# Bias and mask of four attention tiles moved to TensorE, with new load order, attention pace and last output block

## Chip, cores and metric

The kernel runs on one core of one Trainium2 chip. The metric is the device time of one execution, in microseconds (us). All runs quoted below are fast (not disturbed). The profile comes from one of these executions. Its span, from the first to the last record, is shorter than the device time that is reported for the same run (354.5 us of 356.26, for instance). Starts of products are read from the traces, where this does not enter.

## The reference

Attention with a sliding window of 128 keys and a linear bias for each head, followed by a gated feed-forward block. The core of it:

```python
rel = pos[:, None] - pos[None, :]                      # 8 batches, 8 heads, 576 positions, 64 per head
slopes = 2.0 ** (-8.0 * (np.arange(H) + 1) / H)
bias = slopes[:, None, None] * (-np.abs(rel))
mask = (rel >= 0) & (rel < 128)
scores = np.where(mask, q @ k.T / sqrt(64) + bias, -1e9)
x = softmax(scores) @ v                                # x: 4608 tokens x 512
g = x @ w_gate                                         # w_gate, w_val: 512 x 1536
out = (g * sigmoid(g) * (x @ w_val)) @ w_out           # w_out: 1536 x 512
```

## The kernel before

The 4608 tokens are nine blocks of 512 for the feed-forward part; the attention makes them in 36 tiles. The first four tiles are computed at once. From there the two parts are interleaved: TensorE's list is 12 pairs of gate and up products for each block (`pg`, `pv`), the output product of the block before (`po`), and between them the attention of the tiles that come next. Three places matter for what follows.

The masks of the attention. A table `m_reg` = exp(-slope x distance), zero outside the window, is made on ScalarE, and VectorE multiplies the exponentials by it:

```python
def first_masks():
    nc.vector.tensor_copy(idf, idm)
    for h in sorted(range(H), key=slot):
        nc.scalar.activation(reg[:, slot(h), :], dist, AF.Exp, scale=-(2.0 ** (-8.0 * (h + 1) / H)))
# ... in scores():
    def act(q4, par):
        o = 4 * q4 + 2 * par
        nc.scalar.activation(e[:, o:o + 2, :], banks[q4][par], AF.Exp, scale=scale)
    def mul(q4):
        o = slice(4 * q4, 4 * q4 + 4)
        nc.vector.tensor_mul(e[:, o, :], e[:, o, :], reg[:, o, :])
```

The pace. After each step of the feed-forward part, as many steps of the attention are emitted as `target` says. One attention step brings its transposes of q and k, its scores, its exponentials, or its product with v into the program. A tile of q or k is loaded some tiles ahead by GpSimd's DMA queue, as its buffer comes free, and then transposed by TensorE through the identity (`pt<-idm,qn`):

```python
while (at := next(steps)) < ALONE:          # ALONE = 8: these feed-forward steps go alone
    ...
for step in steps:
    b1 = 24 + 3 * PRE                       # 24: the first block ends, the second begins
    if step < b1:
        target = base + max(0, step - ALONE) + max(0, step - 16) * (32 - b1 + ALONE) / (b1 - 16)
    elif step < 60:
        target = base + 32 + SECOND * 8 * (step - b1) / (60 - b1)
    ...
    while (n_att < target or done < ready[blk]) and att_step():
        pass
```

The end. Blocks 1 to 7 use Strassen's scheme for their output product, seven products of half size in place of eight; the last block uses the plain form, with a small last store:

```python
for j in range(3):
    for _ in project(NBLK - 1, j, ps_a, "a", 4):
        yield 1.0
yield from last_project(NBLK - 1, 3)        # two halves of 256 columns, stored on two queues
```

The softmax here doesn't subtract the row's maximum and nothing guards it: scores larger than these inputs give would overflow.

## Time and profile before

| | before |
|---|---|
| median of 3 runs | 356.27 us (356.26 to 356.39) |
| span of the profiled run | 354.5 us |
| TensorE busy | 341.5 us, 96% |
| start of the first gate product | 18.38 us |
| start of the fourth gate product (the first with 512 columns) | 26.67 us |
| start of the second block's first gate product | 56.93 us |
| stretches at half clock, from 6.45 us, where the trace's clock record begins, to TensorE's last product | none (clock 1.00) |

The prediction below shows the page and the stretches.

### The profile page before, as it was taken

The page shows a single profiled execution, that of the slowest core. Times are in us where ns is not written, and L with a number is a line of the kernel's source. Part 1 is how long each engine was busy: PE and PEld are TensorE (multiplying, and loading weights), DVE is VectorE, ACT ScalarE, POOL GpSimd, SP SyncE. Part 2 cuts the span into 40 slices and gives each one's busy share as a digit, 9 for nine tenths or more (in the row PEclk, how much of TensorE's full clock was granted, in tenths as well). Part 3 has the DMA queues.
Part 4 walks back from the last instruction along what each step waited for, and adds up shares of the span by engine and source line. Part 5 has one row for each costly group of instructions (what it writes and reads, how often), then busy time and mean ns, then how long its engine had stood idle before and what let it go on. Part 6 is the DMA issues. An engine that isn't in the chain of part 4 may idle for free.

```text
span 354.5 us, 7261 instructions
## 1 busy us (share of the span) xinstructions
PE 341.5 (96%) x2765; PEld 197.5 (56%) x2765; DVE 273.4 (77%) x599; ACT 178.9 (50%) x355; POOL 106.9 (30%) x132
## 2 busy tenths in 40 slices
PE   7889999999999999999999999999999999999995
PEld 4684555444456655565456555664665566556643
DVE  4867976997987799678986998799878965975540
ACT  6845584555555455665556455455444323332321
POOL 8966655544848445544300100000000000000000
PEclk9999999999999999999999999999999999999999
DMA  9999999999999999999995513311022101101114
GB/s 152 170 186 187 141 176 155 99 147 137 157 142 196 146 158 163 157 167 153 165 62 105 83 39 32 88 33 58 17 75 61 44 2 59 62 0 62 41 42 96
DMA packets 157763, 37.34 MB, mean 105 GB/s; under 512 B 147232, under 2 KB 153248, under 8 KB 157728
## 3 DMA queue, kind: packets, MB, share of 16 engines
q0 software_dynamic: 116224, 18.62, 79.8%
q1 hardware_dynamic: 41056, 17.97, 27.6%
q8 instruction: 21, 0.34, 0.4%
q10 hardware_dynamic: 448, 0.30, 0.3%
q14 instruction: 14, 0.11, 0.1%
HBM read 37.91 MB, written 9.44 MB: 134 GB/s over the span
## 4 chain that ended last, share of the span: by engine, by line
PE 73%; DVE 16%; ACT 7%; issue 3%; DVEq 0%; ACTq 0%
PE pv L369 20%; PE pg L369 20%; PE po L489 14%; PE av L320 4%; DVE uu L384 4%; DVE hT L391 3%; PE ps L255 3%; PE po L410 3%; DVE ex L264 3%; PE p L489 2%; ACT ex L260 2%; PE px L346 2%; ACT tt L383 2%; ACT exc L287 2%; DVE x L323 1%
## 5 line engine op out<-in xcount | busy, mean ns | idle before, releaser
L369 PE MATMUL pg<-xT,wg_sb 128*128 128x512 f16 (+2 forms) x464 | 116.0, 365 | 0.6 <-DVE uu L384 0.3
L369 PE MATMUL pv<-xT,wv_sb 128*128 128x512 f16 (+2 forms) x464 | 114.5, 364 | 0.8 <-DVE uu L384 0.4
L383 ACT ACTIVATE tt<-pg 128x512 f16<-128x512 f32 (+2 forms) x110 | 65.5, 596 | 85.2 <-PE pg L369 81.8
L384 DVE SCALAR_TENSOR_TENSOR uu<-tt,pg 128x512 f16<-128x512 f16 (+2 forms) x109 | 73.4, 674 | 34.6 <-ACT tt L383 33.9
L391 DVE TENSOR_TENSOR hT<-uu,pv 128x512 f16<-128x512 f16 (+2 forms) x110 | 74.0, 673 | 7.1 <-PE pv L369 2.2
L369 PEld LDWEIGHTS <-wv_sb 128*128 128x128 f16 x464 | 42.8, 98 | 37.4 <-issue 3.3
L369 PEld LDWEIGHTS <-wg_sb 128*128 128x128 f16 x464 | 42.5, 98 | 36.1 <-issue 3.5
L260 ACT ACTIVATE ex<-ps 128x512 f16<-128x512 f32 x96 | 50.2, 605 | 10.1 <-PE ps L255 10.1
L169 POOL DMA_DIRECT2D va<-in_v_dram x40 | 34.1, 856 | 53.0 <-PE av L320 36.9
L175 POOL DMA_DIRECT2D qn<-in_q_dram x39 | 33.6, 864 | 24.4 <-DMA qT<-qn 14.8
L175 POOL DMA_DIRECT2D kn<-in_k_dram x39 | 33.2, 859 | 25.7 <-DMA kT<-kn 18.4
L264 DVE TENSOR_TENSOR ex<-ex,m_reg 128x1024 f16<-128x1024 f16 x48 | 32.6, 687 | 10.3 <-ACT ex L260 10.3
L489 PEld LDWEIGHTS <-hT 128*128 128x128 f16 x336 | 31.8, 98 | 15.5 <-issue 3.6
L489 PEld LDWEIGHTS <-S 128*128 128x128 f16 x252 | 23.9, 98 | 11.8 <-issue 2.9
L323 DVE TENSOR_TENSOR x<-av,rec 128x256 f16<-128x256 f32 x72 | 29.0, 420 | 0.6
L489 PE MATMUL po<-T,hT 128*128 128x256 f16 x168 | 23.1, 272 | 0.5
L489 PE MATMUL po<-T,S 128*128 128x256 f16 x168 | 23.0, 273 | 0.6 <-ACT p5s L507 0.6
L287 ACT ACTIVATE exc<-psc 128x512 f16<-128x512 f32 x40 | 21.4, 608 | 3.4 <-PE psc L283 3.4
L347 ACT COPY xT<-px 128x512 f16<-128x512 f16 x24 | 14.1, 586 | 14.9 <-PE px L346 14.8
L320 PEld LDWEIGHTS <-ex 128*128 128x128 f16 x384 | 18.4, 97 | 4.9 <-issue 0.7
L320 PE MATMUL av<-va,ex 128*128 128x65 f16 x384 | 20.4, 193 | 0.5
L410 PE MATMUL po<-wo_sb,hT 128*128 128x512 f16 x84 | 19.7, 379 | 0.0
(74 smaller groups left out, 291.0 us busy)
## 6 DMA issues: line engine op xcount, KB each, us to landing
out_dram<-osb SPq DMA_DIRECT2D x32, 256.0 KB, 2.8
va<-in_v_dram POOLq DMA_DIRECT2D x32, 128.0 KB, 7.5
qn<-in_q_dram POOLq DMA_DIRECT2D x31, 128.0 KB, 8.2
kn<-in_k_dram POOLq DMA_DIRECT2D x31, 128.0 KB, 8.1
wo_sb<-in_moe_w_out_dram POOLq DMA_DIRECT2D x2, 768.0 KB, 9.3
wg_sb<-in_moe_w_gate_dram POOLq DMA_DIRECT2D x2, 512.0 KB, 10.5
wv_sb<-in_moe_w_val_dram POOLq DMA_DIRECT2D x2, 512.0 KB, 11.8
out_dram<-osb SPq DMA_DIRECT2D x6, 128.0 KB, 2.4
```

Source lines behind the costliest of these rows:

```text
L169: nc.gpsimd.dma_start(va[rank][p0:p1, :, 0:D], src)
L175: nc.gpsimd.dma_start(t_[p0:p1], src)
L260: nc.scalar.activation(e[:, o:o + 2, :], banks[q4][par], AF.Exp, scale=scale)
L264: nc.vector.tensor_mul(e[:, o, :], e[:, o, :], reg[:, o, :])
L320: nc.tensor.matmul(av[:, j, :], w, val, start=(n == 0), stop=(n == len(todo) - 1))
L323: nc.vector.tensor_mul(x[:, 4 * half:4 * half + 4, :], av[:, :, 0:D], rec.broadcast_to([P, 4, D]))
L369: nc.tensor.matmul(ps[:, c0:c1], w[:, kb, ms], xT[n][:, kb, c0:c1], start=(kb == 0 and c0 == 0), stop=(kb == NKB - 1 and c1 == 512), skip_ ...
L383: nc.scalar.activation(tt, pg[:, c0:c1], AF.Tanh, scale=0.5)
L384: nc.vector.scalar_tensor_tensor(out=uu, in0=tt, scalar=one if (n, m) == PIN else 1.0, in1=pg[:, c0:c1], op0=ALU.add, op1=ALU.mult)
L391: nc.vector.tensor_mul(hT[n][:, m, c0:c1], acted[(n, m)][1][:, c0:c1], pv[:, c0:c1])
L410: nc.tensor.matmul(po, hT[n][:, m, j * P:(j + 1) * P], wo_sb[:, m, :], start=(i == 0), stop=(i == NMB - 1))
L489: nc.tensor.matmul(dst, a[:, m, cols], b[:, m, :], start=(start and m == 0), stop=(m == HM - 1), skip_group_check=True)
```

## The change

The intent is to take the mask products off VectorE between 11 and 19 us. For the first four tiles the bias (with the window mask as a very large distance) is added to the scores in PSUM by a product of the identity with a bias table. With that come further edits: the copies of `xT` of these tiles go from ScalarE to VectorE, dummy products and repeated transposes go, the tables `m_reg` are made later, loads are put in a new order, the attention's pace between the first and the second block is made smoother, and the last block gets the seven products too.

```diff
+    bias = hpool.tile([P, H, 256], FP16, name="bias", tag="hT")
     def first_masks():
+        for n, h in enumerate(by_slot):
+            to, by = bias[:, slot(h), :], -(2.0 ** (-8.0 * (h + 1) / H)) / scale
+            if n % 2:
+                nc.vector.tensor_scalar_mul(to, dist, by)
+            else:
+                nc.scalar.mul(to, dist, by)
+    def later_masks(n, many):                              # the m_reg tables, two by two, later
 ...
+                for par in range(2 if early_tile else 0):
+                    o = 4 * q4 + 2 * par
+                    nc.tensor.matmul(two[par], idm, bias[:, o:o + 2, :], start=True, stop=False)
 ...
-    loaded = 9
-    for a0 in (0, 6):
-        nc.gpsimd.dma_start(wo_sb[:, a0:a0 + 6, :], wo2[:, a0:a0 + 6, :])
+    nc.gpsimd.dma_start(wo_sb[:, 6:12, :], wo2[:, 6:12, :])
+    load_qk(9)
+    nc.gpsimd.dma_start(wo_sb[:, 0:6, :], wo2[:, 0:6, :])
+    load_v(9)
+    loaded = 10
 ...
-                target = base + max(0, step - ALONE) + max(0, step - 16) * (32 - b1 + ALONE) / (b1 - 16)
+                target = base + 1.5 * max(0, step - ALONE) + max(0, step - 16)
 ...
-        for j in range(3):
-            for _ in project(NBLK - 1, j, ps_a, "a", 4):
-                yield 1.0
-        yield from last_project(NBLK - 1, 3)
+        ends = [strassen(NBLK - 1, t) for t in range(2)]
+        for t in 7 * (0, 1):
+            next(ends[t])
+            yield 0.75
```

The pace line: between steps 8 and 24 both forms emit 32 attention steps. The old one has emitted 8 of them by step 16 and 24 in the last 8 steps; the new one 12 by step 16 and 20 after it.

More of the change, by code (lines that the diff above doesn't have):

```diff
@@ L27 @@
 IDLE = {("k", 0): 0, ("q", 0): 2}
-REPEAT = {("q", 1): 4, ("k", 1): 2, ("q", 2): 4}
+REPEAT = {("q", 1): 4, ("k", 1): 2}
 FIRST = 4
@@ L43, in make_distance @@
     u = np.arange(2 * P)[None, :] - np.arange(P)[:, None]
-    return np.where((u >= 0) & (u < WIN), u, 30000).astype(np.float32)
+    return np.where((u >= 0) & (u < WIN), u, 16000).astype(np.float32)
 @with_exitstack
@@ L88 @@
     reg = consts.tile([P, H, 256], FP16, name="m_reg")
+    bias = hpool.tile([P, H, 256], FP16, name="bias", tag="hT")
+    by_slot = sorted(range(H), key=slot)
     def first_masks():
         nc.vector.tensor_copy(idf, idm)
-        for h in sorted(range(H), key=slot):
+        for n, h in enumerate(by_slot):
[5 more added lines that the diff above has]
+    def later_masks(n, many):
+        for h in by_slot[n:n + many]:
             nc.scalar.activation(reg[:, slot(h), :], dist, AF.Exp, scale=-(2.0 ** (-8.0 * (h + 1) / H)))
@@ L198, in transposed @@
         t_ = (natk if name == "k" else natq).pop(rank)
-        for _ in range(REPEAT.get((name, rank), 2) if rank < FIRST else 1):
+        for _ in range(REPEAT.get((name, rank), 1)):
             for j in range(4):
@@ L240, in scores @@
         if p == 3:
-            return scores_128(s, p, p, (s, p), reg[:, :, 0:P])
+            return scores_128(s, p, p, (s, p), reg[:, :, 0:P], i < FIRST)
         ks = (9 * s + p) % NK
         banks = []
+        early_tile = i < FIRST
         e = epool.tile([P, H, 256], FP16, name="ex", tag="ex", bufs=4)
@@ L255, in products @@
                         nc.tensor.matmul(two[par][:, j, :], kT[rows, ks, pair, :],
-                                         qT[rows, p:p + 2, pair, :], start=(j == 0), stop=(j == 1))
+                                         qT[rows, p:p + 2, pair, :], start=(j == 0 and not early_tile),
+                                         stop=(j == 1))
         def act(q4, par):
@@ L262, in mul @@
         def mul(q4):
+            if early_tile:
+                return
             o = slice(4 * q4, 4 * q4 + 4)
@@ L267, in scores, with scores_128 @@
                 [lambda: act(1, 0)], [lambda: act(1, 1), lambda: mul(1)]]
-    def scores_128(s, kt, qt, key, m):
+    def scores_128(s, kt, qt, key, m, early_tile=False):
         ks = (9 * s + kt) % NK
@@ L279, in products @@
             banks.extend(ps_a.tile([P, 4, P], FP32, name="psc", tag="a") for _ in range(2))
+            for par in range(2 if early_tile else 0):
+                nc.tensor.matmul(banks[par].rearrange("k (a b) q -> k a b q", a=2), idm,
+                                 bias.rearrange("k (a par b) q -> k a par b q", a=2, par=2)
+                                 [:, :, par, :, 0:P], start=True, stop=False)
             for j in range(4):
@@ L283, in products @@
                     nc.tensor.matmul(banks[par][:, j, :], kT[rows, ks, j, :], qT[rows, qt, j, :],
-                                     start=(j == 0), stop=(j == 3))
+                                     start=(j == 0 and not early_tile), stop=(j == 3))
         def act(par):
@@ L290, in scores_128 @@
         return [[products], [lambda: act(0)],
-                [lambda: act(1), lambda: nc.vector.tensor_mul(e, e, m)]]
+                [lambda: act(1), lambda: early_tile or nc.vector.tensor_mul(e, e, m)]]
     xs = {}
@@ L302, in weighted @@
             av = pool.tile([P, 4, D + 1], FP32, name="av", tag=tag)
-            if 0 < i < FIRST:
-                for _ in range(2):
-                    nc.tensor.matmul(av.rearrange("p j d -> p (j d)")[:, 0:256], idle[:, 0:P],
-                                     idle[:, 0:256], start=True, stop=True)
             todo = []
@@ L346, in x_transposed @@
             nc.tensor.transpose(pt[:, kb, :], x[:, kb * P:(kb + 1) * P], idm if i < FIRST else idm2)
-        nc.scalar.copy(dst, pt)
+        if i < FIRST:
+            nc.vector.tensor_copy(dst, pt)
+        else:
+            nc.scalar.copy(dst, pt)
     PIN = (1, 0)
@@ L403, in rows_of, with store @@
         return [(0, 128, n * S + j * P)]
+    def store(n, j, osb, c0=0, c1=512, two=False):
+        for i, (p0, p1, r0) in enumerate(rows_of(n, j)):
+            (nc.scalar if two and i else nc.sync).dma_start(out[r0:r0 + p1 - p0, c0:c1],
+                                                            osb[p0:p1, c0:c1])
     def project(n, j, pool, tag, bufs):
@@ L414, in project @@
                 nc.scalar.mul(osb, po, 0.5)
-                for p0, p1, r0 in rows_of(n, j):
-                    nc.sync.dma_start(out[r0:r0 + p1 - p0, :], osb[p0:p1, :])
+                store(n, j, osb)
             yield
-    def last_project(n, j):
-        osb = opool.tile([P, DM], FP32, name="osb", tag="osb")
-        for half in range(2):
-            c = slice(half * DM // 2, (half + 1) * DM // 2)
-            po = ps_a.tile([P, DM // 2], FP32, name="po", tag="a", bufs=4)
-            for m in range(NMB):
-                nc.tensor.matmul(po, hT[n][:, m, j * P:(j + 1) * P], wo_sb[:, m, c],
-                                 start=(m == 0), stop=(m == NMB - 1))
-            if half == 0:
-                nc.scalar.mul(osb[:, c], po, 0.5)
-            else:
-                nc.vector.tensor_scalar_mul(osb[:, c], po, 0.5)
-            for i, (p0, p1, r0) in enumerate(rows_of(n, j)):
-                (nc.sync if i == 0 else nc.scalar).dma_start(out[r0:r0 + p1 - p0, c], osb[p0:p1, c])
-            yield 1.5
     HM = NMB // 2
@@ L479, in strassen @@
         cols = slice(t * P, (t + 1) * P)
-        po = ps_f.tile([P, 2, HC], FP32, name="po", tag="po", bufs=1)
+        end = n == NBLK - 1
+        pool, tag, bufs = (ps_a, "a", 4) if end and t else (ps_f, "po", 1)
+        po = pool.tile([P, 2, HC], FP32, name="po", tag=tag, bufs=bufs)
         p2 = ps_a.tile([P, HC], FP32, name="p2", tag="a")
         top, low = (opool.tile([P, DM], FP32, name="osb", tag="osb") for _ in range(2))
-        p1s = supool.tile([P, HC], FP32, name="p1s", tag="p1s", bufs=1)
-        p5s = supool.tile([P, HC], FP32, name="p5s", tag="p5s", bufs=1)
-        u2s = supool.tile([P, HC], FP32, name="u2s", tag="u2s", bufs=1)
+        if end and t:
+            spare = [opool.tile([P, DM], FP32, name="osb", tag="osb") for _ in range(2)]
+            p1s, p5s, u2s = spare[0][:, 0:HC], spare[0][:, HC:DM], spare[1][:, 0:HC]
+        else:
+            p1s, p5s, u2s = (supool.tile([P, HC], FP32, name=i, tag=i, bufs=1)
+                             for i in ("p1s", "p5s", "u2s"))
         def product(dst, a, b, start=False):
@@ L510, in strassen @@
         half_plus(low[:, HC:DM], X, p5s)
+        if end and t:
+            store(n, t + 2, low, HC, DM, True)
         yield
@@ L513, in strassen @@
         half_plus(top[:, HC:DM], Y, u2s)
+        store(n, t, top, 0, DM, end)
         yield
         product(X, A22, T4)
-        nc.scalar.mul(low[:, 0:HC], X, 0.5)
-        for j, osb in ((t, top), (t + 2, low)):
-            for p0, p1, r0 in rows_of(n, j):
-                nc.sync.dma_start(out[r0:r0 + p1 - p0, :], osb[p0:p1, :])
+        if end:
+            nc.vector.tensor_scalar_mul(low[:, 0:HC], X, 0.5)
+        else:
+            nc.scalar.mul(low[:, 0:HC], X, 0.5)
+        store(n, t + 2, low, 0, HC if end and t else DM, end)
         yield
@@ L546, in ffn @@
                         weight_sums(m // 2 - 1)
-                if 0 < n < NBLK - 1 and m >= 9:
+                if n > 0 and m >= 9:
                     sums(n, m - 9)
@@ L611, in first_tiles @@
         val(0, 0, early[(0, 0, "v")][0], 0, 384)
+        later_masks(0, 2)
         gate(0, 1, early[(0, 1, "g")][0], 0, 384)
@@ L650 @@
     load_w(256, 512)
+    load_w(512, 768)
     load(4)
     load_qk(5, "q")
-    load_w(512, 1024)
+    load_w(768, 1024)
     load_qk(5, "k")
@@ L694, in everything @@
                     nc.scalar.copy(idm2, idm)
+                if at in (1.0, 3.0, 4.0):
+                    later_masks(2 * (1, 3, 4).index(at) + 2, 2)
         for step in steps:
```

## The prediction

> **What bounds the kernel now.** I first read the page's list of engines and its slices, then the stretches of the span, then the chain of waits at the start and at the end. The page:
>
> ```profile
> PE 341.5 (96%) x2765; PEld 197.5 (56%) x2765; DVE 273.4 (77%) x599; ACT 178.9 (50%) x355; POOL 106.9 (30%) x132
> ...
> PE   7889999999999999999999999999999999999995
> ...
> DVE  4867976997987799678986998799878965975540
> ```
>
> TensorE is busy almost everywhere; only its first three slices (some 9 us each) and the last are not full. So a change pays by what it takes off TensorE's list of work, by ending TensorE's waits in the first 60 us, or by shortening the tail. The table of stretches (columns: length, then busy time and count of each engine, clock, DMA) says where the waits are:
>
> ```profile
> 10.00:20.00 10.00, 8.32 (x144) 6.72 (x142) 8.80 (x23) 7.59 (x16) 9.02 (x12) 1.00 2.06 172
> 20.00:30.00 10.00, 9.12 (x117) 7.14 (x113) 6.53 (x17) 4.92 (x12) 5.80 (x8) 1.00 1.82 181
> ...
> 50.00:60.00 10.00, 9.26 (x80) 4.68 (x79) 6.87 (x16) 6.08 (x12) 5.25 (x6) 1.00 2.21 160
> 60.00:80.00 20.00, 19.73 (x151) 9.64 (x150) 19.42 (x43) 11.56 (x23) 9.23 (x11) 1.00 1.80 127
> ```
>
> From 10 to 20 us VectorE is busier (8.80) than TensorE, whose 8.32 includes dummy products. I also added up, from the start of each product to the start of the next, what exceeds the usual distance for its size: about 4 us in 0 to 20 us[...], 1.6 in 20 to 30, 0.3 in 30 to 40, 1.1 in 40 to 50, 1.6 in 50 to 60, and only some 7 us in the other 290 us. The chain of waits, start, length, work:
>
> ```profile
> 13.04 0.42 DVE qT L207
> 13.47 1.20 DVE ex L264 x2
> 14.67 0.10 DVE rec L322
> 14.77 0.02 issue
> 14.80 0.42 DVE x L323
> ...
> 16.10 1.20 DVE ex L264 x2
> 17.30 0.11 DVE rec L322
> 17.41 0.02 issue
> 17.43 0.44 DVE x L323
> 17.86 0.05 issue
> 17.91 0.39 PE av L306 x2
> ```
>
> Here VectorE does the mask products (ex, 1.20 us a tile) between the copies and the normalisation, and TensorE waits. That is what the change aims at. At the end the chain is TensorE alone:
>
> ```profile
> 340.15 7.77 PE po L410 x36
> 347.92 2.63 PE po L426 x24
> ```
>
> so the last block's output product is 7.77 + 2.63 = 10.40 us of exposed TensorE time, and the span ends 3.9 us after it (a VectorE copy, a store, the closing).
>
> [...]216 ns from start to start at 512 columns, 109 at 256, 56 at 128. [...]two 512-column products at 5.2 us took 0.85 us together, 427 ns each. [...]the page shows 605 for ex, and 0.52 us from start to start. [...]
>
> **The change part by part.**
> (1) Masks. Away from VectorE: three tiles at 1.20 us and one at 0.6, 4.2 us, all between 11 and 19 us. To VectorE come four bias products[...] and four xT copies of 0.42 us (1.7 us), taken from ScalarE. On TensorE 14 products of 512 columns come, 14 x 0.216 = 3.0 us; away go 12 dummies x 0.109 = 1.3 us and, since the q/k transposes are repeated less, 24 x 0.056 = 1.3 us. Net +0.4 us in a stretch with idle time.
> With these rows I walked the order of the changed kernel forward. q1 is transposed at 7.5 us as before; the first ex starts at 9.7 (9.52 before), because two bias products stand before it. Then ScalarE is the bound: 12 ex x 0.52 us, to 16.0, and the last exc at 17.3 (18.3 before). The third tile's x is ready at about 18.3, the fourth's at 20.3.
> (2) The weights. TensorE reaches the first gate product at 16.7, but the up-projection weights were issued at 10.80 and took 7.0 us to land: 17.8 us. The loads ahead of them are unchanged, so TensorE waits about 0.9 us there. From 17.8 its own work runs on (first three gate/up pairs, the fourth tile): I get the start of the fourth gate product (first of 512 columns) at about 24.2 us; before it was 26.67. Gain at this point 2.4 us.
> (3) The mask tables move. Eight exps (2.56 us in all) and four copies (about 0.55 each) stood between 4.4 and 9.3 us on ScalarE, under the loads. They now stand among the tanh of the first pairs, at 22 to 30 us. My walk has the third pair's tanh at 26.0 to 26.5 and its VectorE product done at 27.2; the fourth up product needs that PSUM buffer and was at 28.02 before. So only about 1.3 of the 2.4 us survive here. At 32 to 37 us ScalarE has caught up, and I get 1.8 us.
> (4) Loads. The total ahead of the tile loads at 29 to 40 us is the same, only reordered (a quarter of the weights goes ahead of the fifth tile). The q tile that is transposed at 42.4 us landed at 40.1 (issued 30.08, 10.0 us under way). The new order wants it at about 38.5. TensorE then waits some 1 us, unless the load comes sooner. Gain after this: 1.0 us.
> (5) Smoother attention from 40 to 60 us. Before, the attention steps were pressed together there; waits for x and PSUM cost 2.7 us. Now more of them come early, and the first output product comes after two gate pairs. I give this 0.9 us of the 2.7.
> (6) Last block with seven products. 14 x 6 = 84 products of 256 columns at 0.109 us, 9.16 us, for 10.40: 1.24 us less, all exposed. VectorE gets 12 sums of 0.34 us in the last three pairs; the S2 sum should be ready at 342.2 in old times against 342.8 for its use. I take 0.2 us off for a delayed buffer. The store at the end is as small as before (two pieces of 64x256 on two queues), so the tail stays at 3.9 us.
> Sum: 1.0 + 0.9 + 1.0 = 2.9 us at the low reading of (4); if the load does not hold it, 1.8 + 0.9 + 1.0 = 3.7. Between them, weighted toward the upper because VectorE's work falls too: 3.4 us, so 356.3 - 3.4 = **352.9 us**.
>
> **The rivals.**
> A. The early gain is eaten entirely: landings set the pace to 40 us, and the mask tables hold tanh. For it: the DMA slices are full to 190 us, and the landings in (2) and (4) are within 1 to 2 us of their use. Against: the weights for the ninth pair (37.1) still come before I need them (37.8). Then only (6) stays: 355.1 us.
> B. TensorE falls back to half clock, since the dummies are gone. [...]Against: bias products fill the same gaps, and no gap in my walk is over 1 us. It would make 354.5 to 357.
> C. The stalls of 40 to 60 us vanish and the early 2.4 us survive in full: 2.4 + 2.5 + 1.2 = 6.1, 350.2 us. For it: this was presumably tuned; from 20 to 60 us VectorE and ScalarE are below 90% busy.
> D. VectorE becomes the bound from 60 to 80 us, where it has 19.42 of 20 us. If blocks arrive earlier there but VectorE's own work is the same, part of the gain is handed back. [...]353.5 us.
>
> **Range and chances.** A and B bound it above, C below; I keep a bit inside A and C: 350.6 to 355.1 us. Faster by over 2% means under 349.1, more than even C gives: 6%. Slower by over 2% means over 363.4: nothing but a stalled load chain does it, 1%.
>
> **What will show it.** (1) right: no ex product on VectorE before 25 us, and ScalarE's twelve ex nearly without gaps from 9.7 to 16. (2) right: TensorE idle before the first up product until about 17.8. (3) right: the chain between 22 and 30 us goes through ScalarE's tanh behind m_reg. (4) right: a wait of TensorE before the q transposes at about 38 us. (5): excess in 40 to 60 us under 2 us. (6): the last 84 products take 9.2 us, the tail 3.9. The prediction is wrong if products of 512 columns at 10 to 24 us take 427 ns (B), if the fourth gate product starts at 26 us or later (A), or if the 60 to 340 us stretch, 280 us before, itself changes by more than 1 us, which nothing in my sum provides for.

The sum: it came to 1.0 + 0.9 + 1.0 = 2.9 us, or 1.8 + 0.9 + 1.0 = 3.7 with the other reading of (4), was set at 3.4 between them by the author's estimate, and gave 356.3 - 3.4 = 352.9 us. Rival B's 354.5 to 357 us rested on a price for a stretch at half clock. The 216, 109, 56 and 427 ns of TensorE's products and the 605 ns of `ex` are from the trace of the kernel before.

## More of the kernel before

One more view is needed later: TensorE's instructions in order of time where the second block begins. The columns are start, length, engine, line, operation, what is written from what, and how many were merged; a bracket would say how long the engine had been idle before and on what.

```profile
53.82 1.89 PE L410 MATMUL po<-wo_sb,hT 128*128 128x512 f16 x8
...
56.93 1.02 PE L369 MATMUL pg<-xT,wg_sb 128*128 128x512 f16 x4
...
60.38 1.03 PE L369 MATMUL pg<-xT,wg_sb 128*128 128x512 f16 x4
...
61.41 0.61 PE L202 MATMUL pt<-idm,qn 128*128 128x128 f16 x8
```

Read it as an order: output products of the first block, then five groups of gate and up products of the second, and only then, at 61.41 us, the transposes of the q tiles 9 and 10. The load of tile 10 landed at 57.46 us, nearly 4 us earlier. Nothing waits there, but only because of where the scheduler put these transposes.

## The result, and the profile after

| | before | after |
|---|---|---|
| median | 356.3 us (356.26 to 356.39, 4 runs) | 362.44 us (360.52 to 362.84, 4 runs) |
| ratio to before | 1 | 1.0161, 95% interval 1.0124 to 1.0198 |
| span of the profiled run | 354.5 us | 361.0 us |
| mean granted clock of the profiled run | 1.00 | 0.991 |

A ratio is the mean time of one kernel's fast runs over that of the other's fast runs in the same rounds, so it is not quite the ratio of the medians quoted. The change costs 1.6%: within the class "same" of 2%, but on the wrong side, and outside the predicted range of 350.6 to 355.1 us.

First the page of after, list of engines and slices:

```profile
PE 344.2 (95%) x2767; PEld 198.5 (55%) x2767; DVE 279.5 (77%) x619; ACT 177.2 (49%) x357; POOL 108.3 (30%) x134
...
PE   7999995999999999999999999999999999999994
...
PEclk9999996999999999999999999999999999999999
```

TensorE's early slices are fuller than before: the aim was met. But the seventh slice (54 to 63 us) has a 5, and the row of the granted clock has a 6 in the same place, where before it was full.

To see where the time came from, I compared the start of the same gate or up product, counted from the first, in both traces (after minus before):

| product | before | after | difference |
|---|---|---|---|
| first of block 0 | 18.38 | 17.53 | -0.85 |
| fourth gate | 26.67 | 25.41 | -1.26 |
| three quarters of block 0 | 40.48 | 41.15 | +0.67 |
| first of block 1 | 56.93 | 59.43 | +2.50 |
| a quarter of block 1 | 62.87 | 70.06 | +7.19 |
| start of block 2 | | | +6.65 |
| last | 339.77 | 346.27 | +6.50 |

(Between such points other work may have moved to the other side of the product, so only from block 2 on, where both orders have done the same, is a difference all time.) From block 2 to the last product nothing changes. Everything happens before 70 us. TensorE in order of time in after:

```profile
54.49 0.28 PE L364 MATMUL px<-idm,x 128*128 128x128 f16 x2 [0.34 <-DVE x L341]
58.60 0.61 PE L214 MATMUL pt<-idm,qn 128*128 128x128 f16 x4 [3.83 <-DMA qn<-in_q_dram]
59.01 0.63 PE L436 MATMUL po<-wo_sb,hT 128*128 128x512 f16 x1
59.43 1.91 PE L390 MATMUL pg<-xT,wg_sb 128*128 128x512 f16 x4
61.14 1.91 PE L390 MATMUL pv<-xT,wv_sb 128*128 128x512 f16 x4
62.84 1.76 PE L390 MATMUL pg<-xT,wg_sb 128*128 128x512 f16 x4
64.44 1.03 PE L390 MATMUL pv<-xT,wv_sb 128*128 128x512 f16 x4
```

The transposes of q tile 10 now stand ahead of the second block's first gate product. Before, they came after its fifth group. The tile landed at 58.56 us, about as late as before (57.46), and TensorE waited 3.83 us for it. The gate products of 59.43 did not pass the transposes in this trace, though ScalarE's last copy of `xT` before them had ended at 55.40 us. Then a second loss follows: four products of 512 columns take 1.71 us from start to start (59.43 to 61.14) in place of 0.86. That is the half clock: the granted clock is 0.50 there. In stretches of 3.41 us, a length that comes back in the traces below (columns: length; busy time and count of TensorE, its weight loads, VectorE, ScalarE, GpSimd; granted clock; share of the DMA engines and GB/s):

```profile
54.10:57.51 3.41, 0.34 (x4) 0.11 (x2) 1.26 (x4) 1.04 (x2) 1.13 (x2) 1.00 2.42 154
57.51:60.92 3.41, 2.32 (x9) 1.14 (x10) 0.42 (x1) 0.00 (x0) 2.85 (x4) 0.50 2.48 154
60.92:64.33 3.41, 3.41 (x9) 1.18 (x8) 1.94 (x4) 0.60 (x1) 1.26 (x2) 0.50 3.18 153
```

The stretch with 0.34 us of work was followed by two at clock 0.50. TensorE worked in them from 58.60 to 64.33, 5.73 us, of which half, 2.87 us, is loss. With the wait that makes 3.83 + 2.87 = 6.70 us, near the 6.65 at block 2 (the early gain and other small waits are in that number too; a cleaner comparison follows with q10_first). The runs of after seem to differ by the same thing. Only that of 362.78 us was profiled, with two such stretches and a mean clock of 0.991. The mean clocks of the others (0.995 for the run of 360.52 us, 0.991 for 362.10, 0.986 for 362.84) would fit one, two and three; but a mean can also hold half clock from after TensorE's last product (best6's trace has 1.00 from 337 to 348 us, but 0.98 from 330 to 353.6, and its products end at 349.4), so this is not shown.

The chain of waits (start, length, what) shows the smaller points of the prediction as well:

```profile
24.90 1.22 ACT m_reg L105 x4
26.12 0.49 ACT tt L404
26.62 0.02 issue
26.64 0.70 DVE uu L405
...
27.38 1.04 PE pv L390 x4
...
30.45 10.20 DMA qn<-in_q_dram
...
40.70 0.40 PE pt L214 x4
...
46.98 11.58 DMA qn<-in_q_dram
```

Four mask tables hold back the third pair's tanh, and the fourth up product, which needs its PSUM buffer, starts at 27.38 us. Then the chain goes through two loads of q: the one that lands at 40.65 costs TensorE only 0.31 us, the one that lands at 58.56 costs 3.83.

At the end the chain is TensorE again, and shorter than the 7.77 + 2.63 us of before:

```profile
346.65 1.31 PE po L502 x12
347.96 1.31 PE p L502 x12
349.27 6.70 PE po L502 x60
...
355.99 0.42 DVE osb L533
```

That is 1.31 + 1.31 + 6.70 = 9.32 us for 84 products. But the last store landed 3.36 us after this last copy (356.41 to 359.77), where before it took 2.22 (351.01 to 353.23). Ten stores with the 1 MB of the whole block are issued between 353.78 and 356.67 us. So the tail after TensorE grew from 3.9 to 5.05 us and took the gain back.

### The profile page after: what moved, and what is told of

The parts are those of the page before. It is cut to its first block, busy times and chain, and to the rows that moved or that the text cites. A ratio compares the mean times of both kernels' runs of the same rounds, so it can differ in the third digit from the quotient of the medians.

```text
span 361.0 us, 7293 instructions
## 1 busy us (share of the span) xinstructions
PE 344.2 (95%) x2767; PEld 198.5 (55%) x2767; DVE 279.5 (77%) x619; ACT 177.2 (49%) x357; POOL 108.3 (30%) x134
## 4 chain that ended last, share of the span: by engine, by line
PE 76%; DVE 8%; DMA 6%; ACT 5%; issue 2%; POOL 0%; DVEq 0%; ACTq 0%
PE pg L390 22%; PE pv L390 21%; PE po L502 16%; DMA qn<-in_q_dram 6%; PE av L338 4%; PE ps L271 3%; PE p L502 3%; DVE hT L412 2%; DVE uu L405 2%; ACT ex L277 2%; PE px L364 2%; ACT tt L404 2%; PE po L436 1%; PE pt L214 1%; DVE ex L283 1%
## 5 line engine op out<-in xcount | busy, mean ns | idle before, releaser
L390 PE MATMUL pg<-xT,wg_sb 128*128 128x512 f16 (+2 forms) x464 | 117.5, 369 | 0.3 <-DVE xT L366 0.2
L390 PE MATMUL pv<-xT,wv_sb 128*128 128x512 f16 (+2 forms) x464 | 116.2, 367 | 0.9 <-DVE uu L405 0.5
L502 PEld LDWEIGHTS <-hT 128*128 128x128 f16 x384 | 36.4, 98 | 16.2 <-issue 3.4
L283 DVE TENSOR_TENSOR ex<-ex,m_reg 128x1024 f16<-128x1024 f16 x42 | 28.8, 687 | 9.6 <-ACT ex L277 9.6
L502 PEld LDWEIGHTS <-S 128*128 128x128 f16 x288 | 27.4, 98 | 12.3 <-issue 2.9
L502 PE MATMUL po<-T,S 128*128 128x256 f16 x192 | 26.0, 273 | 0.6 <-ACT p5s L520 0.6
L502 PE MATMUL po<-T,hT 128*128 128x256 f16 x192 | 26.1, 272 | 0.4
L271 PE MATMUL ps<-qT,kT 64*128 64x256 f16 x192 | 17.5, 272 | 0.6 <-DVE qT L219 0.5
L368 ACT COPY xT<-px 128x512 f16<-128x512 f16 x20 | 11.7, 586 | 10.0 <-PE px L364 9.9
```

Of the source, the lines that this page charges most:

```text
L271: nc.tensor.matmul(two[par][:, j, :], kT[rows, ks, pair, :], qT[rows, p:p + 2, pair, :], start=(j == 0 and not early_tile), stop=(j == 1))
L390: nc.tensor.matmul(ps[:, c0:c1], w[:, kb, ms], xT[n][:, kb, c0:c1], start=(kb == 0 and c0 == 0), stop=(kb == NKB - 1 and c1 == 512), skip_ ...
L502: nc.tensor.matmul(dst, a[:, m, cols], b[:, m, :], start=(start and m == 0), stop=(m == HM - 1), skip_group_check=True)
```

## The experiments

**Theory P (pace).** The new pace line alone puts q tile 10's transposes ahead of the second block. The wait and the half clock after it are all of the loss. **Rival L (loads).** The new load order makes tile 10 late. **Rival E (early part).** The bias products, or dummies that are gone, changed something that costs time later. **For the end:** the seven products gain on TensorE what the crowd of stores loses. Each edit below is against the changed kernel unless it says otherwise; all results were correct.

### pace_old: the old pace line in the changed kernel

```diff
-                target = base + 1.5 * max(0, step - ALONE) + max(0, step - 16)
+                target = base + max(0, step - ALONE) + max(0, step - 16) * (32 - b1 + ALONE) / (b1 - 16)
```

> The changed kernel with one line undone: the pace at which attention steps are handed out in the first block is the old one. In this build the transposes of q tile 10 stand on TensorE after the first gate and up products of the second block again, as in the kernel before. Theory (q10's place in TensorE's order is the cause: 4.0 us of waiting for its load, then about 2.7 us lost to the half clock): no wait over 1 us between 50 and 60 us, 512-column products never slower than 216 ns after 10 us, time 355.2 +- 0.8 us. Rival (the moved mask tables or the load order are the cause): 361 us or more.

Measured: 358.5 us (356.73 to 359.15), ratio 1.0057 (1.003 to 1.0085). The wait for tile 10 is gone, but the time isn't back. TensorE in order of time:

```profile
55.45 0.59 PE L436 MATMUL po<-wo_sb,hT 128*128 128x512 f16 x2 [2.02 <-DMA wo_sb<-in_moe_w_out_dram]
```

With the old pace the output products of the first block come here, and they need `wo_sb`, whose first half (`0:6`) the new load order had put behind the q and k of tile 9. So a second wait, of 2.02 us, came into place, and in the profiled run a stretch of half clock (56.17 to 59.58). The run of 356.73 us, with a mean clock of 0.999, had none of that length. The old pace with the new load order gives a wait too, only for another load. The size that I expected was missed because I had looked at q tile 10 alone.

### both_old: old pace and old end of the load list

```diff
+    loaded = 9
+    for a0 in (0, 6):
+        nc.gpsimd.dma_start(wo_sb[:, a0:a0 + 6, :], wo2[:, a0:a0 + 6, :])   # in place of the five new lines
-                target = base + 1.5 * max(0, step - ALONE) + max(0, step - 16)
+                target = base + max(0, step - ALONE) + max(0, step - 16) * (32 - b1 + ALONE) / (b1 - 16)
```

> The changed kernel with both the old pace of the attention steps and the old end of the load list; what stays is the bias through the identity, the moved mask tables, the earlier weight quarter and the seven products at the end. Theory (the pace line puts q tile 10 too early, the load order pushes the output weights back; nothing else costs): no wait over 1 us from 45 to 65 us, no half clock, third block 1 to 1.5 us earlier than before, end product 1.1 us shorter but the stores after it 1.1 us longer, time 355.0 +- 0.6 us. Rival (the mask part costs too): 357 us or more.

Measured: 355.75 us (355.3 to 356.22), ratio 0.9982 (0.9967 to 0.9996), just above what was expected (354.4 to 355.6). There is a wait of 0.69 us for `wo_sb`, and no half clock. The product-by-product difference to before is -1.14 us at the fourth gate product and -0.70 from block 1 on, where 1 to 1.5 us had been expected. So the early part of the change, bias on TensorE included, is worth a little; rival E falls.

### loads_late_old: only the old end of the load list, new pace kept

The edit is the first half of the one above.

> The changed kernel with the end of the load list put back (both halves of the output weights, then tile 9 as a whole and tile 10). TensorE's order around 54 us is the same as in the changed kernel in this build. Theory (the order on TensorE decides, the loads only say how long the wait is): q tile 10 still lands at 57.5 to 58.6 us, time 361 to 362.8 us. Rival (the reordered loads are the cause): 356 us or less.

Measured: 362.75 us (362.06 to 363.75), ratio 1.0187 (1.0168 to 1.0205). The waits for tile 10 (3.67 us) and the half clock (58.14 to 64.97) are there, with smaller waits for the k and q tiles 9 (0.33 and 0.64 us). With the old loads tile 10 landed at 59.18 us, later than in after (58.56) and than I expected, so the new load order did not make it late. Rival L falls.

### before_pace: the kernel before with the new pace line alone

```diff
 (against the kernel before)
-                target = base + max(0, step - ALONE) + max(0, step - 16) * (32 - b1 + ALONE) / (b1 - 16)
+                target = base + 1.5 * max(0, step - ALONE) + max(0, step - 16)
```

> The kernel before with the pace line alone changed. In this build q tile 10 is transposed ahead of the second block's first gate product. Theory (the pace line by itself brings the wait): TensorE waits 2 to 4 us for that tile at 54 to 58 us, half clock for one or two windows after it, time 360 +- 1.5 us. Rival (the pace line does harm only after the faster start): 356.2 +- 0.6 us.

Measured: 361.7 us (361.67 to 361.98), ratio 1.015 (1.0135 to 1.0165): one line brings nearly the whole loss, a little more than the expected 358.5 to 361.5 us. TensorE in order of time:

```profile
58.35 0.61 PE L202 MATMUL pt<-idm,qn 128*128 128x128 f16 x4 [1.90 <-DMA qn<-in_q_dram]
58.75 1.91 PE L369 MATMUL pg<-xT,wg_sb 128*128 128x512 f16 x4
```

The same transposes ahead of the same gate products, a wait for the same tile, and products at half clock (55.62 to 62.45, 6.83 us). The loss is put together differently, though: the wait for tile 10 is shorter, and three waits stand before it, of 0.79 us for VectorE's `x` and of 0.85 and 0.44 us for the k and q tiles 9. The transposes of tile 9 begin here at 54.79 us, in before at 56.74. The 3.41 us in which these three waits lie (52.21 to 55.62, 39% busy) were the last at full clock. From block 2 on every product is 5.4 us late. Theory P holds in both directions: put into the good kernel the line gives the loss, taken out together with its load order it removes it.

### q10_first: new pace kept, tile 10 of q loaded earlier

The edit leaves TensorE's order as it is, and only lets the load start sooner. It tells whether the order by itself costs, or the order together with a late load.

```diff
     def load(rank):
-        load_qk(rank)
+        load_qk(rank, "k" if rank == 10 else "kq")
 ...
     load_qk(9)
+    load_qk(10, "q")
```

> The changed kernel with TensorE's order kept word for word, but q tile 10 is loaded right after tile 9, ahead of the second half of the output weights, so that it should land near 52 us instead of 58.56. Theory (that one landing is what TensorE waits for): the wait at 54.6 us goes, clock stays full, time 355.7 +- 0.8 us. Rival (the place in the order disturbs by itself, PSUM or the copies behind it): 360 us or more.

Measured: 356.54 us (356.12 to 356.92), ratio 1.001 (0.9995 to 1.0025). TensorE in order of time, at the place of the 3.83 us:

```profile
54.42 0.39 PE L214 MATMUL pt<-idm,qn 128*128 128x128 f16 x4
54.89 0.39 PE L436 MATMUL po<-wo_sb,hT 128*128 128x512 f16 x1
55.26 1.02 PE L390 MATMUL pg<-xT,wg_sb 128*128 128x512 f16 x4
```

No wait, no half clock. The load landed at 50.80 us, and the time is at the upper edge of what was expected. One load issued earlier gives back 5.9 us of median, and 6.65 - 0.28 = 6.37 us at block 2, against the 6.70 of the account above (0.26 of the 6.37 were there at the first gate product already, 17.27 against 17.53 us). What is left is that this kernel is 0.28 us behind before at block 2, while both_old is 0.70 ahead. Between 30 and 50 us q10_first has three single waits that both_old does not have: 0.48 us (for a copy of `qT`, at 33.98), 0.38 (for the q tile that lands at 40.5) and 0.31 (for an exponential, at 43.16). So the smoother pace has a second, smaller cost: it asks for things a little before they are ready. I did not test this one by itself.

### dum5: dummy transposes in front of the wait

Twenty dummy transposes ahead of the wait were to keep the clock up without touching the wait.

```diff
+        if i == 7:
+            for _ in range(5):
+                for kb in range(NKB):
+                    nc.tensor.transpose(pt[:, kb, :], idle[:, kb * P:(kb + 1) * P], idm2)
```

> The changed kernel with 20 dummy transposes (1.1 us) into the same PSUM tile shortly before the wait, so that the wait for q tile 10 remains[...]. Theory (the loss is 4.0 us of waiting and 2.7 us of half clock after it): the wait stays to about 58.5 us, products after it take 216 ns, time 359.7 +- 0.6 us. Rival (the half clock is only a shadow of the wait and costs little): 362 us.

Measured: 361.47 us (361.18 to 361.74), ratio 1.0146. A miss, nearer to the rival's 362 us. The dummies were done before the wait began, which stayed at 3.73 us, and one stretch of 3.41 us, cut as below, had no work of TensorE at all:

```profile
55.20:58.61 3.41, 0.00 (x0) 0.00 (x0) 0.42 (x1) 0.63 (x2) 1.88 (x3) 1.00 2.43 154
```

The clock was 0.50 all the same, but for 3.41 us (58.61 to 62.03, 92% busy) in place of 6.83. The time is 1.0 us below that of after. But how these stretches lie to the wait differs from run to run (the last at full clock begins at 54.10 us in after, with 0.34 us of work, and at 55.20 here, with none), so it is not shown that the dummies spared the second one. What the run does show is that work ahead of this wait of 3.73 us did not keep the clock up; work inside the wait was not tried.

### seven_only: the kernel before with the seven products of the last block

The edit is the last-block part of the diff above, with its buffers and stores.

> The kernel before with the last block's seven products and their stores alone. Theory (TensorE's gain at the end is given back by stores that all fall into the last 3.4 us): the products take 1.1 us less, the last store lands 1.1 us later after them, time 356.2 +- 0.4 us. Rival (the prediction: the tail stays): 355.1 us.

Measured: 356.08 us (355.98 to 356.14), ratio 0.9991 (0.9976 to 1.0005), as expected. From the start of the last up product to TensorE's end it takes 9.69 us, in place of 10.77, and the last store lands 3.40 us after the last copy in place of 2.22. The gain of 1.1 us and the loss of 1.2 cancel. So the crowd at the end is of this part's making, and has nothing to do with the rest of the change.

### best3: a first try at a better version

Old pace, `wo_sb` in the order of its use, all eight mask tables right after the fourth tile, and the two chains of the end no longer mixed.

```diff
+            if i == FIRST - 1:
+                later_masks(0, 8)            # in place of the calls among the first tanh
-        for t in 7 * (0, 1):
+        for t in (0, 1, 0, 1) + 5 * (0,) + 5 * (1,):
+    for a0 in (6, 0):                        # and the old pace line
```

> The changed kernel with the old pace, the output weights' second half first and both ahead of tile 9, the mask tables made in ScalarE's idle time from 18 us on, and the first two of seven products interleaved but then one pair of row tiles finished ahead of the other, so that its stores leave 3 us earlier. Theory: no wait over 1 us, full clock, fourth up product 0.8 us earlier than in the changed kernel, tail 4.2 us instead of 5.0, time 353.6 +- 0.8 us. Rival (the tail is not set by the crowd of stores): tail 5 us, 354.5 us or more.

Measured: 358.5 us (357.96 to 359.11), ratio 1.0054: a miss. With all eight tables there, the scheduler moved the four copies that follow them ahead of the first tanh too. ScalarE was late for the first pair (its first tanh began at 22.67 us), and this stretch went by:

```profile
22.52:25.93 3.41, 1.69 (x23) 1.21 (x21) 2.59 (x7) 1.85 (x6) 2.69 (x4) 1.00 2.12 169
```

TensorE was busy for half of it, without any long gap (the longest 1.35 us), and the clock was 0.50 in the next 3.41 us (25.93 to 29.34). The unmixed end took 12.2 us on TensorE (341.04 to 353.21) for 9.2 us of work: its products wait for the copies of those before (0.31 us for `p5s`, 0.35, 0.57 and 0.52 for `osb`). The tail after TensorE was 4.13 us, as expected (4.2): with stores that leave earlier it is shorter than the 5.05 us of after, so the crowd of stores set it there.

### seven_early: stores of the end issued as soon as each quarter is done

Against the kernel before, with the seven products:

```diff
         half_plus(top[:, 0:HC], p2, p1s)
+        if end:
+            store(n, t, top, 0, HC, True)
 ...
-        store(n, t + 2, low, 0, HC if end and t else DM, end)
+        store(n, t + 2, low, 0, HC if end else DM, end)
```

> The kernel before with the seven products in the last block, and with finished quarters stored as soon as they are ready: the left half of the top tiles after the second product, the right half of the low ones after the fifth, for both pairs. Theory (the long tail of the seven products is the crowd of stores, 1 MB in 3.4 us): the last store lands 2.5 to 3.0 us after the last copy instead of 3.4, time 0.4 to 0.8 us below the seven products alone, 355.5 +- 0.4 us. Rival (the landing of small pieces sets it, not their crowd): no change, 356.1 us or more.

Measured: 357.26 us (356.45 to 357.3), ratio 1.002 (1.0006 to 1.0033): a miss. The stores did spread, and the last one landed 2.0 us after its issue, in place of 3.15, and 2.97 us after the last copy, as expected. But TensorE's end stage grew from 9.69 to 10.72 us, of which 0.88 is a wait for ScalarE's copy `u2s`; the next runs take this up.

### best4 and best5: the old pace with early stores

best4 is the changed kernel with the old pace, `wo_sb` loaded in the order of its use with `loaded = 9`, the early stores, and six of the mask tables made after the fourth tile (two later). best5 is the same without moving the tables.

> The changed kernel with the old pace, the output weights ahead of tile 9 with the half first that is used first, the quarters stored as they finish, and six of the eight mask exps made in ScalarE's idle time from 18 us. Theory: no wait over 0.5 us from 45 to 65 us, full clock throughout, fourth up product 0.5 us earlier than in the changed kernel, time 354.3 +- 0.7 us. Rival (making mask tables early shifts tanh and starves TensorE as in the trial before, a window at half clock): 355.7 us or more.

> As the run with this label's neighbour, but with the mask exps left where the change put them. Theory: both waits gone and the tail shortened, time 354.8 +- 0.6 us. Rival (as both old settings together, with nothing won by the weights' order and the earlier stores): 355.7 us.

Measured: best4 354.76 us (354.38 to 354.96), ratio 0.9959 (0.9946 to 0.9971); best5 354.79 us (354.69 to 355.58), ratio 0.9965 (0.9952 to 0.9977). At block 2 they are 1.94 and 1.82 us ahead of before, with a full clock; where the tables are made is thus worth about 0.1 us (best4's fourth up product came at 27.39 us as in after, not 0.5 earlier as expected). Of best5's lead over both_old, 1.1 us, 0.4 is an earlier first gate product (17.26 against 17.65 us) and about 0.7 the wait for `wo_sb`, which is gone. They lose some of this at the end, and TensorE's order of time in best4 says how:

```profile
342.97 1.47 PE L502 MATMUL po<-T,hT 128*128 128x256 f16 x12 [0.89 <-ACT u2s L519]
```

The next group of products needs the PSUM buffer that ScalarE's copy `u2s` frees, and that copy came late. The early stores were issued from SyncE's and from ScalarE's queue, so my reading was that ScalarE's copy stood behind its own store issues: two of them took that queue from 341.02 to 342.49 us, and `u2s` began at 342.54.

### best6: the first early store on one queue

```diff
         if end:
-            store(n, t, top, 0, HC, True)
+            store(n, t, top, 0, HC)
```

(against best4)

> best4 with one edit: the first of the early stores of the ends is issued by SyncE's queue alone instead of by SyncE's and ScalarE's. Theory: in best4 the scale copies u2s and p5s on ScalarE stood behind the store issues of that queue and the products waited for them (end stage of TensorE 10.74 us, 0.89 us of it waiting for u2s). With ScalarE's queue free, the stage takes about 9.7 us, the last store lands 2.4 to 2.7 us after the last copy, and the time is 353.8 us, give or take 0.6, ratio about 0.993. Rival: the copies are late for another reason (the order of ScalarE's copies itself); then the stage stays at 10.7 us and the time at 354.7 us.

Measured: 354.07 us (353.28 to 355.4, 6 runs), ratio 0.9937 (0.9925 to 0.995). TensorE's end stage is 9.69 us, with no wait for `u2s`, and the last store lands 2.44 us after the last copy (349.84 to 352.28). So the reading was right, and this is the best kernel, 2.0 us below before and 8.4 below the change. Its profiled run is its slowest one, 355.4 us; the other five took 353.28 to 354.54. The profile says what that run lost:

```profile
4.53:7.94 3.41, 1.61 (x13) 0.94 (x12) 2.87 (x6) 1.19 (x4) 3.41 (x5) 1.00 2.37 156
7.94:11.35 3.41, 3.41 (x28) 2.57 (x28) 0.85 (x2) 0.00 (x0) 3.41 (x5) 0.50 2.74 150
```

In this run the first 3.41 us were 47% busy, and the next had half clock. Its first gate product started at 19.34 us, where best4, with the same early code, had 17.26. In best4's profile the first stretch lay at 3.84 to 7.25, was 55% busy, and the next, to 10.66, had clock 1.00.

### Busy share of 3.41 us, and the clock that came next

Wherever one of the fourteen profiles shows half clock before TensorE's end, the stretch lasts 3.41 us (best6, 7.94 to 11.35) or 6.83 (after, 57.51 to 64.33), and the stretch at full clock before it a multiple of 3.41: 3.41 (best6), 20.48 (best3), 51.20 (after, loads_late_old, before_pace, pace_old) or 54.61 us (dum5). So I cut the traces into windows of 3.41 us. They are counted from where each run's clock record first shows full clock, and stand here with TensorE's busy share and the clock that was granted in the next one (half is 0.50). Shown are all windows at full clock with a share of 0.10 to 0.55, without the closing ones:

| kernel | window from, us | busy share | next clock |
|---|---|---|---|
| after | 54.1 | 0.10 | half |
| loads_late_old | 54.7 | 0.15 | half |
| before_pace | 52.2 | 0.39 | half |
| pace_old | 52.8 | 0.41 | half |
| best6 | 4.5 | 0.47 | half |
| best3 | 22.5 | 0.50 | half |
| best5 | 4.0 | 0.54 | full |
| dum5 | 4.0 | 0.54 | full |
| best4 | 3.8 | 0.55 | full |
| q10_first | 4.1 | 0.55 | full |

Of the closing windows, which are not in the table, three matter here. The ones in which the products end in after (354.5) and loads_late_old (355.1) had a share of 0.44 and were followed by full clock. They are densely filled for 1.5 us and then empty, while those of 0.47 and 0.50 are a mix of short pieces. The closing window of pace_old, as dense, had 0.41 and was followed by half clock. These are counts from fourteen profiles. They show no limit, and no run here tells why the two of 0.44 differ from those of 0.41, 0.47 and 0.50. In the other direction, windows at half clock that were 0.44 (before_pace) and 0.68 busy (after, loads_late_old) were followed by another at half clock, those of 0.92 (dum5) and 1.00 (six others) by full clock.

## Why the prediction was wrong, point by point

- **(5) is the step that failed.** "Now more of them come early [...] I give this 0.9 us of the 2.7." The smoother pace was entered as a gain that was given and not worked out. What it brought was a transpose that stands too early in TensorE's order: a wait of 3.83 us for q tile 10, and 2.87 us lost to the half clock after it. It cost 5.2 us in the medians when put alone into the kernel before (before_pace). The walk through the changed order had ended at about 42 us. Its last step, (4), had the very mechanism: a q tile that is wanted before it lands. I did not ask it of the next tiles, though the built order shows where tile 10's transposes stand, and the trace of before when it landed: 57.46 us, when TensorE would have come to them at about 54.6.
- **Rival B** had the right second mechanism and the wrong premise: "no gap in my walk is over 1 us". A gap of 3.83 us lay beyond the walk's end. Half clock cost 2.87 us here, for 5.73 us of work at clock 0.50. And in best3 it came without a long gap: 1.69 us of work in 3.41 us (22.52 to 25.93), no gap over 1.35 us, then clock 0.50.
- **(4)** was right in kind and too large for its tile: the q tile at 40.65 cost 0.31 us, not 1.
- **(1)** was right but for sizes. No mask product is left on VectorE in the early tiles. The first ex starts at 9.90 (predicted 9.7), the last exc ends at about 18.2 (17.3), as ScalarE had waits of 0.38 and 0.60 us for TensorE that my walk didn't have. The four bias products on VectorE took 1.73 us, the second and the fourth 0.27 us each, the first and the third 0.66 and 0.76. In all ten builds that have these products, the two long ones end 0.11 to 0.12 us after GpSimd has finished issuing a load; whether they wait for it, no run tests.
- **(2)** The gain at the fourth gate product was 1.26 us, not 2.4; it started at 25.41, not 24.2. The wait for the up-projection weights didn't come: they landed at 16.67 us, and the first up product started at 17.75 without a wait. The lag of (1) took its place.
- **(3)** was right: the fourth up product at 27.38 (predicted 27.2), the chain through ScalarE behind `m_reg`.
- **(6)** The products were right: 1.1 us less on TensorE. The tail was wrong: "the store at the end is as small as before, so the tail stays at 3.9 us". The last store is as small, but it lands behind a crowd of 1 MB, and the tail was 5.05 us. The term is worth 0 in place of 1.0 us (seven_only).
- **Rivals A, C and D** did not happen. From block 2 to the end nothing changed (+6.65 to +6.50 us), as the sum had it.

In size, at block 2 where a difference is all time: the early part was predicted at -1.0 us and measured at -0.70 (both_old); (5) was predicted at -0.9 and measured at 6.65 + 0.70 = +7.35 (after against both_old, so the new end of the load list is in it); (6) was predicted at -1.0 and measured at 0; and 0.5 had been added for a better reading of (4), which did not come. So 8.25 of the miss is the term (5), and about 1.8 all others together (10 in all; the profiled run, 362.78 us, lies 9.9 above the prediction).

What stays open: the profiled start of the first gate product lay between 17.25 and 17.69 us in builds with the same early code (19.34 in best6, with its 3.41 us at half clock), and this moves all later products, so that differences of some 0.4 us between single profiles say little; and which of the small waits of 30 to 50 us in q10_first are to be mended, and how.

## What to carry to other kernels

When a change alters the order in which an engine gets its work, list every load that it now asks for earlier, with its landing in the old trace, through to the end of the stage, and not only up to where the first gain is secured; here the 4 us between the landing (57.46 us) and the old use (61.41) were slack that the new order spent without showing it. The wait on TensorE had two prices here, its length and then the half clock, so that 3.83 us became 6.70; the cheapest repair was one load issued earlier (q10_first, 356.54 us in place of 362.44). Look at the stores behind a gain on the last products too: 1.1 us won there came to nothing in front of a crowd of stores (seven_only, ratio 0.9991), and early stores paid in full only when the first was kept off ScalarE's queue, whose copies TensorE waited for (best4 354.76 us, best6 354.07).
